# Routed experts in a fused attention, mixture-of-experts and MLP kernel: experts ranked by their rows, four of them as 128-row tiles of plain fp32 products

## The chip, the cores and the metric

One core of a Trainium2 chip runs the whole kernel. The metric is the device time of one execution in microseconds; lower is better. Engines are named as in the profile: PE (TensorE products; PEld its weight loads), DVE (VectorE), ACT (ScalarE), POOL (GpSimd), SP (SyncE, which here only issues DMAs).

## The reference

Three stages follow each other: windowed attention with sink columns (2 batches, 8 heads, 768 positions, head size 64), a top-1 mixture of 8 experts over the 1536 rows, and an MLP with a mish-like activation. The middle one is what the change touches:

```python
e_idx = np.argmax(x @ w_gate, axis=1)              # x: 1536 x 512
for e in range(8):                                 # w1: 8 x 512 x 1024, w2: 8 x 1024 x 512
    mask = e_idx == e
    h = np.maximum(x[mask] @ w1[e], 0.0)
    out[mask] = gate_w[mask, None] * eom[mask, e, None] * (h @ w2[e])
h = out @ w_in; g = h * np.tanh(softplus(h)); return g @ w_out    # d_ff 2048
```

All is fp32. With the inputs that the reference draws, the eight experts get 290, 123, 98, 163, 117, 165, 92 and 488 rows; the first 128 rows of expert 0 are computed ahead of the others, which leaves 162 of it.

## The kernel before

**Attention and routing.** `fast()` computes the attention of a pair of heads at a time; `place` scatters each row, scaled by its gate, into a DRAM `table` with an area for each expert (POOL, L337). `rank` leaves `left`, the rows of each expert that are still to be done. On DVE L845 to L891 then pick the expert with the most rows, put it last, and make the integer tables `uni` (weight offsets, table row and output position of each unit) and `lasti`. Meanwhile `pre_chunk` computes 128 rows of expert 0 by plain fp32 products (L790, L798) and splits expert 0's weights (L212 on ACT, L214 on DVE). Then all engines branch on `more`, the number of tiles beyond the planned ten (0 here).

**Experts.** `experts_and_mlp` runs ten tiles of 192 rows: units 0 to 6 have one tile, unit 7, the largest, three. A fp32 product is made of three fp32r products: weights and rows are each split into a high and a low part (ACT copies to fp32r, DVE subtracts: L1117 and L1111 for weights, `split_x` for rows). In `tile_mm` each weight block of 128x128 is used twice: its high part with 384 columns (rows' high and low, L956 and L973), its low part with 192 (L959, L975). `first(b)` makes two blocks of the hidden layer, `second(b)` adds them into `Y`; `put` copies `Y` to `yT`.

**Weights.** A unit's weights are eight pieces of 512 KB: RAW[0..3] are 128 rows of w1 (rows of 4 KB), RAW[4..7] 256 rows of w2 (rows of 2 KB). Each tile has eight `slot`s; the list `jobs` says which piece is split in which slot. `low()` subtracts the low part of the piece before, and then `fetch` loads the same piece of the next unit into the RAW buffer that is now free. SP issues DMAs strictly in the order written. The order of PE, ACT and DVE is written out by hand (`manual_schedule`).

**MLP.** For each of 48 blocks, `in_mm` does 12 products into one bank of a two-bank tile H2, `sigm` (L1254) is the first of the activation's steps on ACT, and `out_mm` (L1231) follows three blocks later. The first two blocks run inside the last tile.

Of the kernel before, what the change touches and what calls it, by code (L numbers as in the profile page):

```python
# [12 lines left out]
F32 = mybir.dt.float32  # L13
# [10 lines left out]
P = 128  # L24
# [3 lines left out]
E = 8  # L28
# [12 lines left out]
NX = 7  # L41
# [3 lines left out]
def tile_kernel(  # L45
# [103 lines left out]
    nc.gpsimd.iota(cap7, [[W, NX]], base=W, channel_multiplier=0, allow_small_or_imprecise_dtypes=True)  # L149
# [616 lines left out]
    W2S += pairs4(wp, "wc")  # L766
    psH = ctx.enter_context(tc.tile_pool(name="mpsH", bufs=1, space=PSUM))
# [9 lines left out]
    def pre_chunk():  # L777
# [29 lines left out]
        place(1, 3, NB - 3, True)  # L807
        hps.append(bank2()[:, 0])
# [23 lines left out]
    with tc.manual_schedule(engines={ET.PE, ET.Activation, ET.DVE}):  # L832
# [7 lines left out]
        extra = mid.tile([P, E], F32, name="extra")  # L840
        em = mid.tile([P, 1], F32, name="em")
        big = mid.tile([P, 1], F32, name="big")
        cd = mid.tile([P, E], F32, name="ecd")
        isem = const.tile([P, E], F32, name="isem")
        v_.tensor_reduce(big, left[:, 1:E], AX.X, ALU.max)  # L845
        v_.scalar_tensor_tensor(cd[:, 1:E], left[:, 1:E], big, id8[:, 1:E], ALU.is_ge, ALU.mult)
        v_.tensor_reduce(em, cd[:, 1:E], AX.X, ALU.max)
        v_.tensor_scalar(big, big, float(W), None, ALU.is_gt)
        v_.scalar_tensor_tensor(em, em, float(1 - E), big, ALU.add, ALU.mult)
        v_.tensor_scalar(em, em, float(E - 1), None, ALU.add)  # L850
        v_.tensor_scalar(isem, id8, em, None, ALU.is_equal)
        key = mid.tile([P, E], F32, name="key")
        v_.scalar_tensor_tensor(key, isem, float(E), id8, ALU.mult, ALU.add)
        v_.tensor_tensor(t64, key.unsqueeze(2).to_broadcast([P, E, E]), key.unsqueeze(1).to_broadcast([P, E, E]),
                         ALU.is_gt)
        v_.tensor_tensor(t64, t64, tot.unsqueeze(1).to_broadcast([P, E, E]), ALU.mult)
        v_.tensor_reduce(off, t64, AX.X, ALU.add)
        v_.tensor_tensor(st_, off, early, ALU.add)
        need = const.tile([P, E], F32, name="need")
        v_.scalar_tensor_tensor(need, isem, -float((LT_ - 1) * W), left, ALU.mult, ALU.add)  # L860
        v_.tensor_tensor(m7, need.unsqueeze(2).to_broadcast([P, E, NX]), cap7.unsqueeze(1).to_broadcast([P, E, NX]),
                         ALU.is_gt)
        v_.tensor_reduce(extra, m7, AX.X, ALU.add)
        v_.tensor_reduce(big, extra, AX.X, ALU.add)
        v_.tensor_copy(cnti, big)
        stc = const.tile([P, E], F32, name="stc")
        v_.tensor_copy(stc, st_)
        ext = const.tile([P, E], F32, name="ext")
        v_.tensor_copy(ext, extra)
        eu = mid.tile([P, E], F32, name="eu")  # L870
        v_.scalar_tensor_tensor(eu, id8, em, id8, ALU.is_ge, ALU.add)
        v_.tensor_copy(eu[:, E - 1:E], em)
        unf = mid.tile([P, E, 4], F32, name="unf")
        v_.tensor_scalar(unf[:, :, 0], eu, float(DM), None, ALU.mult)
        v_.tensor_scalar(unf[:, :, 1], eu, float(FF), None, ALU.mult)
        v_.tensor_scalar(unf[:, :, 2], eu, float(CAP), None, ALU.mult)
        v_.tensor_tensor(t64, id8.unsqueeze(1).to_broadcast([P, E, E]), eu.unsqueeze(2).to_broadcast([P, E, E]),
                         ALU.is_equal)
        v_.tensor_tensor(t64, t64, st_.unsqueeze(1).to_broadcast([P, E, E]), ALU.mult)
        v_.tensor_reduce(unf[:, :, 3], t64, AX.X, ALU.add)  # L880
        v_.tensor_copy(unf[:, 0, 3:4], st_[:, 0:1])
        v_.tensor_copy(uni, unf)
        rl = mid.tile([P, LT_], F32, name="rl")
        v_.tensor_tensor(cd, isem, left, ALU.mult)
        v_.tensor_reduce(big, cd, AX.X, ALU.add)
        v_.tensor_scalar(big, big, -float(W), 0.0, ALU.add, ALU.max)
        v_.tensor_scalar(rl, cap7[:, 0:LT_], -float(W), big, ALU.add, ALU.min)
# [11 lines left out]
    def experts_and_mlp(extra):  # L899
# [6 lines left out]
        rows = rest.enter_context(tc.tile_pool(name="rows", bufs=1))  # L906
        nrm = [rows.tile([P, 512, 2], I32, name=f"nr{c}") for c in range(2)]
        nt = [rows.tile([P, 512], F32, name=f"nt{c}") for c in range(2)]
# [10 lines left out]
        HW = W // 2  # L919
        XS = xp.tile([P, NP, 2, W], F32R, name="XS")  # L920

        def load_x(row, xr=None):
            if xr is None:
                xr = xrp.tile([HW, 2, DM], F32, name="xr")
            first["x"] = nc.sync.dma_start(out=xr, in_=table[ds(row, W), :].rearrange("(p t) f -> p t f", t=2))
            return xr

        def split_x(xr):
            pt = bank2()
            for t in range(2):  # L930
                for d in range(NP):
                    nc.tensor.transpose(pt[:, t, d * HW:(d + 1) * HW], xr[:, t, d * P:(d + 1) * P], ident[0:HW, 0:HW])  # L932
            xs_ = XS.rearrange("p d s (c t) -> p d s t c", t=2)
            pv_ = [pt[:, t, 0:NP * HW].rearrange("p (d c) -> p d c", c=HW) for t in range(2)]
# [5 lines left out]
        def put(pos):  # L940
            for c in range(2):
                t = tb.tile([P, 2, W], F32, name="t")
                nc.scalar.activation(t, Y[c][:, :, W:2 * W], AF.Copy)
                nc.vector.tensor_tensor(yT[:, 2 * c:2 * c + 2, ds(pos, W)], Y[c][:, :, 0:W], t, ALU.add)

        def tile_mm(w1s, w2s, nxt, slot):

            hT = {}

            def first(b, i):  # L950
                hp = bank2()
                for f in range(2):
                    fb = 2 * b + f
                    c = slice(fb * P, (fb + 1) * P)
                    for d in range(NP):
                        nc.tensor.matmul(hp[:, f, 0:2 * W], lhsT=w1s[d][0][:, c], rhs=XS[:, d].rearrange("p s c -> p (s c)"),  # L956
                                         start=(d == 0), stop=False, skip_group_check=True)
                    for d in range(NP):
                        nc.tensor.matmul(hp[:, f, 0:W], lhsT=w1s[d][1][:, c], rhs=XS[:, d, 0],  # L959
                                         start=False, stop=(d == NP - 1), skip_group_check=True)  # L960
                t = tb.tile([P, 2, W], F32, name="t")
                hs = hT[b] = hb.tile([P, 2, 2, W], F32R, name="hs")
                nc.scalar.activation(t, hp[:, :, W:2 * W], AF.Copy)  # L963
                nc.vector.tensor_tensor(t, hp[:, :, 0:W], t, ALU.add)  # L964
# [34 lines left out]
        xr0 = xrp.tile([HW, 2, DM], F32, name="xr")  # L999
        def extra_tiles():  # L1000
# [39 lines left out]
            pick(sj, stc)  # L1040
            v_.tensor_scalar(exf[:, :, 0], ej, float(DM), None, ALU.mult)
            v_.tensor_scalar(exf[:, :, 1], ej, float(FF), None, ALU.mult)
# [3 lines left out]
            v_.scalar_tensor_tensor(exf[:, :, 2], ej, float(CAP), rj, ALU.mult, ALU.add)  # L1046
            v_.tensor_copy(exi, exf)

            def one(j):
                at = [value(exi[0:1, j, c:c + 1], [ET.SP], c) for c in range(3)]  # L1050
                pos = value(exi[0:1, j, 3:4], [ET.DVE], 3)
                xr = load_x(at[2], xr0)
# [4 lines left out]
                split_x(xr)  # L1057
                tile_mm(W1[1], W2S, lambda: None, lambda i: None)
                put(pos)
# [13 lines left out]
        load_x(P, xr0)  # L1073
# [11 lines left out]
        split_x(xr0)  # L1085
# [7 lines left out]
        jobs = []  # L1093
        for t, (u, k_) in enumerate(TILES):
            if u < E - 1:
                jobs += ([(u, p_) for p_ in (5, 6, 7)] if u else [None] * 3) + [(u + 1, p_) for p_ in (0, 1, 2, 3, 4)]
            elif k_ == 0:
                jobs += [(u, p_) for p_ in (5, 6, 7)] + [None, ("n", NA), None, ("n", NA + 1), ("n", NA + 2)]
            elif k_ < LT_ - 1:
                jobs += [("n", NA + 3)] + [(E, p_) for p_ in range(3)] + [("n", NA + 4), (E, 3), ("n", NA + 5), None]  # L1100
# [336 lines left out]
```

## Time and profile before

| | |
|---|---|
| median of 3 runs | 656.57 us (656.41 to 656.68) |
| the profiled execution | 654.65 us, of which the span from first to last instruction is 652.9 |
| PE busy | 610.9 us, 94% of the span |
| tile 0 begins / tile 1 / tile 5 / tile 6 / tile 9 | 173.43 / 194.79 / 270.94 / 290.33 / 347.73 us |
| MLP alone on PE | from 371.74 us |
| DMA traffic | 81.05 MB |

A row of the timeline gives start, duration, engine, line, operation, output<-inputs, shapes and a count; brackets give the engine's idle time just before and what ended it. A merged row covers several instructions. PEclk is the granted TensorE clock: 1.00 is 2.4 GHz, 0.50 is 1.2 GHz.

### The profile page before, as it was taken

The numbers are of one execution on the slowest core, as the hardware profiler recorded it, in microseconds if no ns is written. First come the engines' busy times: TensorE is split into PE (matmuls) and PEld (weight loads), VectorE is DVE, ScalarE is ACT, GpSimd is POOL, SyncE is SP. The second block draws the span as 40 slices with busy tenths as digits, with TensorE's granted clock in tenths as the row PEclk, the third lists the DMA queues.
The fourth block names the chain that finished last, engine by engine and source line by source line (L and its number), as shares of the span: only waits on it lengthen the run. The fifth ranks groups of instructions, "written<-read, shape, count | busy, mean of one in ns | idle before, by whom it ended". The sixth has DMA issues, their size and how long they took to land.

```text
span 652.9 us, 9634 instructions
## 1 busy us (share of the span) xinstructions
PE 610.9 (94%) x3460; PEld 501.8 (77%) x3460; DVE 382.4 (59%) x841; ACT 410.9 (63%) x748; POOL 46.5 (7%) x73
## 2 busy tenths in 40 slices
PE   3999999889599999999999989999899999999995
PEld 2556666565499999999999867777688887888884
DVE  4466669659368788888887777677323133231312
ACT  2666666548167667666455776868767576766752
POOL 3020113304000000000000000000020000200002
PEclk9999999999699999999999989999999999999998
DMA  6789796502668777778331113221010000100001
GB/s 127 180 209 318 223 278 198 186 17 98 222 231 264 248 238 237 254 233 263 118 99 64 65 64 112 81 97 35 1 65 0 1 0 1 64 2 0 2 0 70
DMA packets 66000, 81.05 MB, mean 124 GB/s; under 512 B 42832, under 2 KB 42832, under 8 KB 65936
## 3 DMA queue, kind: packets, MB, share of 16 engines
q1 hardware_dynamic: 63872, 73.97, 37.1%
q0 software_dynamic: 1920, 6.29, 2.4%
q8 instruction: 32, 0.52, 0.3%
q14 instruction: 32, 0.26, 0.2%
q10 hardware_dynamic: 144, 0.00, 0.0%
HBM read 66.88 MB, written 13.37 MB: 123 GB/s over the span
## 4 chain that ended last, share of the span: by engine, by line
PE 65%; issue 15%; DVE 8%; ACT 6%; DMA 2%; POOL 1%; SPq 0%; POOLq 0%; DVEq 0%; ACTq 0%
PE h L1216 14%; PE acc L1231 12%; PE h L956 9%; PE Y L973 8%; PE h L959 5%; PE Y L975 4%; PE pt L305 3%; PE s L308 3%; PE avA L308 3%; DMA nr<-in_moe_w_in_dram 2%; PE pt L308 1%; DVE ms L526 1%; POOL out_dram L1245 1%; PE h L932 1%; ACT p L528 1%
## 5 line engine op out<-in xcount | busy, mean ns | idle before, releaser
L1263 DVE TENSOR_TENSOR fx<-h,fx 128x512 f32<-128x512 f32 x48 | 31.0, 687 | 140.0 <-ACT fx L1260 140.0
L973 PE MATMUL Y<-hs,wch 128*128 128x384 f32 x320 | 94.5, 361 | 0.0
L975 PE MATMUL Y<-hs,wcl 128*128 128x192 f32 x320 | 80.6, 252 | 0.0
L1254 ACT ACTIVATE fx<-h,nln 128x512 f32<-128x512 f32 x48 | 33.1, 689 | 68.5 <-PE h L1216 68.3
L528 ACT ACTIVATE p<-ms,nm 128x272 f32<-128x272 f32 (+1 forms) x96 | 47.3, 494 | 30.8 <-DVE nm L526 30.1
L975 PEld LDWEIGHTS Y<-hs,wcl 128*128 128x128 f32 x320 | 61.1, 191 | 0.1
L973 PEld LDWEIGHTS Y<-hs,wch 128*128 128x128 f32 x320 | 60.1, 188 | 0.1
L526 DVE CUSTOM_DVE_ANT_0 ms<-s,m 128x272 f32<-128x272 f32 (+1 forms) x96 | 36.3, 408 | 23.5 <-PE s L308 19.1
L963 ACT ACTIVATE t<-h 128x384 f32<-128x384 f32 x40 | 19.7, 493 | 42.2 <-PE h L959 41.1
L1216 PE MATMUL h<-yh,wah 128*128 128x512 f32 x96 | 39.0, 406 | 7.4 <-ACT fx L1254 7.4
L1245 POOL DMA_INDIRECT out_dram<-nr,idx x12 | 11.5, 961 | 475.2 <-DVE nr L1241 472.5
L956 PE MATMUL h<-XS,wbh 128*128 128x384 f32 x192 | 42.7, 344 | 0.1
L308 PE MATMUL s<-kT,qT 64*128 64x272 f32 (+1 forms) x192 | 40.0, 454 | 2.1 <-DVE nm L526 2.1
L1216 PE MATMUL h<-yh,wal 128*128 128x512 f32 x96 | 38.5, 401 | 0.0
L1231 PE MATMUL acc<-wdh,gh 128*128 128x512 f32 x96 | 38.0, 395 | 0.0
L1231 PE MATMUL acc<-wdl,gh 128*128 128x512 f32 x96 | 37.9, 394 | 0.0
L964 DVE TENSOR_TENSOR t<-h,t 128x384 f32<-128x384 f32 x40 | 22.3, 557 | 25.7 <-ACT t L963 24.8
L1111 DVE TENSOR_TENSOR wcl<-rax,wch 128x1024 fp32r<-128x1024 f32 x30 | 36.5, 1215 | 0.0
L556 ACT ACTIVATE ph<-pt 128x512 f32<-128x512 f32 (+1 forms) x48 | 24.9, 550 | 16.8 <-PE pt L305 16.8
L1267 ACT ACTIVATE gh<-fx 128x512 fp32r<-128x512 f32 x48 | 29.5, 632 | 5.7 <-DVE fx L1263 5.7
L1271 DVE TENSOR_TENSOR gl<-fx,gh 128x512 fp32r<-128x512 f32 x48 | 31.0, 689 | 2.4
L1117 ACT ACTIVATE wch<-rax 128x1024 fp32r<-128x1024 f32 x30 | 31.7, 1058 | 0.8 <-PE Y L973 0.8
(277 smaller groups left out, 1455.9 us busy)
## 6 DMA issues: line engine op xcount, KB each, us to landing
rax<-in_moe_w_dram SPq DMA_DIRECT2D x56, 512.0 KB, 4.6
nr<-in_moe_w_in_dram SPq DMA_DIRECT2D x16, 512.0 KB, 5.8
nr<-in_moe_w_out_dram SPq DMA_DIRECT2D x16, 512.0 KB, 3.5
table<-zer SPq DMA_DIRECT2D x17, 256.0 KB, 5.9
raw<-in_moe_w_dram SPq DMA_DIRECT2D x8, 512.0 KB, 5.7
xr<-table SPq DMA_DIRECT2D x10, 384.0 KB, 7.1
vr<-in_v_dram SPq DMA_DIRECT2D x16, 192.0 KB, 3.6
kr<-in_k_dram SPq DMA_DIRECT2D x14, 192.0 KB, 3.9
```

Of the source, the lines that this page charges most:

```text
L308: last_pe[0] = nc.tensor.matmul(*args, **kw)
L526: nc.vector.tensor_tensor_reduce(ms[:, 0:w], s[j][:, 0:w], m, 1.0, 3.0e38, ALU.add, ALU.min, nm[:, j, i:i + 1])
L528: nc.scalar.activation(p[:, j, i, o:o + w], ms[:, 0:w], AF.Exp, bias=nm[:, j, i:i + 1], scale=-1.0, accum_out=sm[:, j, i:i + 1])
L956: nc.tensor.matmul(hp[:, f, 0:2 * W], lhsT=w1s[d][0][:, c], rhs=XS[:, d].rearrange("p s c -> p (s c)"), start=(d == 0), stop=False, skip_g ...
L959: nc.tensor.matmul(hp[:, f, 0:W], lhsT=w1s[d][1][:, c], rhs=XS[:, d, 0], start=False, stop=(d == NP - 1), skip_group_check=True)
L973: nc.tensor.matmul(Y[c // 2][:, c % 2, 0:2 * W], lhsT=wh, rhs=hT[b][:, f].rearrange("p s c -> p (s c)"), start=(b == 0 and f == 0), stop=F ...
L975: nc.tensor.matmul(Y[c // 2][:, c % 2, 0:W], lhsT=wl, rhs=hT[b][:, f, 0], start=False, stop=(b == 3 and f == 1), skip_group_check=True)
L1111: nc.vector.tensor_tensor(lo, RAW[p_], hi.bitcast(F32), ALU.subtract)
L1117: nc.scalar.activation(wpair(*j)[0], RAW[j[1]], AF.Copy)
L1216: nc.tensor.matmul(h, lhsT=wt[:, (fb % 8) * P:(fb % 8 + 1) * P], rhs=xx[d], start=(k_ == 0), stop=(k_ == 11))
L1231: nc.tensor.matmul(accs[tb], lhsT=g_[:, tb * P:(tb + 1) * P], rhs=w_[:, c], start=(fb == 0 and k_ == 0), stop=(fb == NF - 1 and k_ == 2))
L1254: nc.scalar.activation(x_, st[n]["h"], AF.Sigmoid, bias=nln2)
```

## The change

The units are ranked on the chip by their rows (`rank_e`): unit 0 stays expert 0, then the others in ascending order; unit 7 is the largest. Units 1 to 4 (`SM`) get one tile of 128 rows each, units 0, 5 and 6 one of 192, unit 7 two of 192 and a last one of 128. Units 1 to 4 are computed by `tile_plain`: plain fp32 products straight from RAW, no splits, and each piece is fetched anew for the next unit as soon as its products are issued. For them a w1 piece is a block of 256 columns of all 512 rows, so that its DRAM runs are 1 KB. The splits of unit 5 move into tile 4. The rows of tile 0 are loaded before the branch (`load_x` in `pre_chunk`). In the MLP the odd block's `in_mm` is told not to depend on the even block's `sigm`. Output positions and ids are made in tiles 0 to 2 rather than 2 to 5. POOL makes a few more small constants at the start.

```diff
+SM = range(1, 5)
+    nrm = [rows.tile([P, 512, 2], I32, name=f"nr{c}") for c in range(2)]
+    xr0 = nrm[0].bitcast(F32).rearrange("p f w -> p (f w)")
...
         place(1, 3, NB - 3, True)
+        load_x(P, W, xr0)
...
+        v_.scalar_tensor_tensor(key, left, float(E), kb, ALU.mult, ALU.add)
+        v_.tensor_tensor(t64, rows_of(key), cols_of(key), ALU.is_gt)
+        v_.tensor_reduce(rank_e, t64, AX.X, ALU.add)
+        v_.tensor_tensor(hot_r, rows_of(id8), cols_of(rank_e), ALU.is_equal)
...
+            elif unit in SM and p < 4:
+                nc.sync.dma_start(out=RAW[p].rearrange("p (d f) -> p d f", d=NP),
+                                  in_=w1f[ds(wat[unit][0], DM), p * 256:(p + 1) * 256].rearrange("(d p) f -> p d f", p=P))
...
+        def tile_plain(u, nxt, slot):
+            def first(b, i):
+                hp = bank2()
+                w_ = RAW[b].rearrange("p (d f) -> p d f", d=NP)
+                for f in range(2):
+                    for d in range(NP):
+                        nc.tensor.matmul(hp[:, f, 0:P], lhsT=w_[:, d, f * P:(f + 1) * P], rhs=XT[:, d],
+                                         start=(d == 0), stop=(d == NP - 1), skip_group_check=True)
+                hT[b] = tb.tile([P, 2, W], F32, name="t")
+                nc.scalar.activation(hT[b][:, :, 0:P], hp[:, :, 0:P], AF.Relu)
+                slot(i)
+                fetch(u + 1, b)
+            def second(b):
+                for f in range(2):
+                    for c in range(NP):
+                        nc.tensor.matmul(Y[c // 2][:, c % 2, 0:P], lhsT=RAW[4 + b][:, f * 512 + c * P:f * 512 + (c + 1) * P],
+                                         rhs=hT[b][:, f, 0:P], start=(b == 0 and f == 0), stop=(b == 3 and f == 1),
+                                         skip_group_check=True)
+                fetch(u + 1, 4 + b)
+            slot(0)
+            first(0, 1)
+            first(1, 2)
+            second(0)
+            first(2, 3)
+            second(1)
+            first(3, 4)
+            slot(5)
+            nxt()
+            second(2)
+            slot(6)
+            second(3)
+            slot(7)
...
-        load_x(P, xr0)
+            load_x(P, W, xr0)
...
+        wide = [P if u in SM or k_ == LT_ - 1 else W for u, k_ in TILES]
+        jobs = {(4, 3 + p_): (5, p_) for p_ in range(5)}
+        for u in (5, 6, 7):
+            jobs.update({(u, i_): (u, 5 + i_) for i_ in range(3)})
+            if u < 7:
+                jobs.update({(u, 3 + p_): (u + 1, p_) for p_ in range(5)})
...
+                if n % 2:
+                    tc.declare_no_dep(mm.ins, st[n - 1]["sg"].ins, reason="the two banks of one tile")
...
+            if u in SM:
+                tile_plain(u, nxt, slot)
+            else:
+                tile_mm(wide[t], W1[u % 2], W2S, nxt, slot)
```

## Rows read from the trace of the kernel before

**Rows 1.** The page, part 1: busy time, share of the span, instructions.

```profile
PE 610.9 (94%) x3460; PEld 501.8 (77%) x3460; DVE 382.4 (59%) x841; ACT 410.9 (63%) x748; POOL 46.5 (7%) x73
```

**Rows 2.** Windows: busy us by engine, PEclk, DMA share, GB/s; tiles 1-4, MLP.

```profile
194.79:270.94 76.15, 76.15 (x547) 76.15 (x545) 64.40 (x97) 52.66 (x80) 0.00 (x0) 1.00 0.79 250
374.70:649.00 274.30, 264.03 (x1117) 209.80 (x1116) 111.29 (x181) 186.43 (x261) 11.53 (x12) 0.99 0.10 34
```

**Rows 3.** Timeline, PE: first product of tiles 0, 1, 5, 6, 9.

```profile
173.43 0.66 PE L956 MATMUL h<-XS,wah 128*128 128x384 f32 x1 [1.40 <-ACT yT L1089]
...
194.79 0.36 PE L956 MATMUL h<-XS,wbh 128*128 128x384 f32 x1
...
270.94 0.36 PE L956 MATMUL h<-XS,wbh 128*128 128x384 f32 x1
...
290.33 0.36 PE L956 MATMUL h<-XS,wah 128*128 128x384 f32 x1
...
347.73 0.41 PE L956 MATMUL h<-XS,wbh 128*128 128x384 f32 x1
```

**Rows 4.** Timeline, PE: plain fp32 products and transposes back to back.

```profile
144.81 0.73 PEld L308 LDWEIGHTS pt<-wx,xT 128*128 128x128 f32 x5
...
145.49 0.49 PEld L305 LDWEIGHTS pt<-ident,xpre 128*128 128x128 f32 x4
...
159.34 3.60 PE L798 MATMUL h<-raw,zer 128*128 128x512 f32 x8
```

**Rows 5.** The chain of work: twelve split (fp32r) products of 512 columns.

```profile
386.06 2.80 PE h L1216 x12
```

**Rows 6.** Windows as in Rows 2: loads in runs of 256 B, then of 2-4 KB.

```profile
10.00:12.00 2.00, 1.41 (x7) 1.00 (x5) 0.00 (x0) 0.49 (x1) 0.00 (x0) 1.00 1.12 249
176.00:182.00 6.00, 6.00 (x35) 6.00 (x35) 1.68 (x3) 1.85 (x4) 0.00 (x0) 0.81 1.04 404
```

**Rows 7.** Pieces of weights: ns of a split's halves; landing of a piece.

```profile
L1117 ACT ACTIVATE wbh<-rax x18: 1047/1052/1059, 183.2 to 366.2; 128x1024 fp32r<-128x1024 f32 x18
...
L1111 DVE TENSOR_TENSOR wbl<-rax,wbh x18: 1203/1219/1223, 185.2 to 377.2; 128x1024 fp32r<-128x1024 f32 x18
...
DMA to landing us min/median/max: 3.5/4.6/9.3
```

**Rows 8.** Timeline: first and last of 36 routing instructions on DVE; the branch.

```profile
150.22 0.15 DVE L845 TENSOR_REDUCE big<-left 128x1 f32<-128x7 f32 x1
...
156.75 0.17 DVE L891 CAST lasti<-lsf 128x6 int32<-128x6 f32 x1
...
161.70 4.63 DVE L214 TENSOR_TENSOR wcl<-raw,wch 128x1024 fp32r<-128x1024 f32 x4
...
166.24 0.69 DVE L1070 COPY nt<-h 128x512 f32<-128x512 f32 x1
166.47 0.35 SPq L925 DMA_DIRECT2D xr<-table  x1
169.05 2.19 SPq L193 DMA_DIRECT2D rax<-in_moe_w_dram  x4
...
169.66 1.51 PE L932 MATMUL h<-ident,xr 96*128 96x96 f32 x8 [6.72 <-DMA xr<-table]
...
172.20 1.02 DVE L938 TENSOR_TENSOR XS<-h,XS 128x384 fp32r<-128x384 f32 x2 [5.27 <-ACT XS L936]
```

**Rows 9.** Windows as in Rows 2: the two stretches at the lower clock.

```profile
168.10:178.30 10.20, 7.24 (x30) 6.90 (x31) 1.02 (x2) 1.64 (x4) 0.00 (x0) 0.50 0.84 290
379.70:383.10 3.40, 3.40 (x10) 2.62 (x9) 3.26 (x7) 0.63 (x1) 0.00 (x0) 0.50 0.39 139
```

**Rows 10.** Waits of PE's weight loads from 374 us (total, times, longest); timeline.

```profile
PEld h L1216 <- ACT fx L1254: 10.9, 9, 4.4
...
378.66 0.50 PE L1216 MATMUL h<-yh,wah 128*128 128x512 f32 x1 [3.94 <-ACT fx L1254]
```

**Rows 11.** Timeline: the first work of PE in the span.

```profile
9.25 0.87 PE L305 MATMUL pt<-ident,kr 128*128 128x128 f32 x3 [9.25 <-DMA kr<-in_k_dram]
```

More of the change, by code (lines that the diff above doesn't have):

```diff
@@ L766, in tile_kernel, with load_x @@
     W2S += pairs4(wp, "wc")
+    rows = ctx.enter_context(tc.tile_pool(name="rows", bufs=1))
+    nrm = [rows.tile([P, 512, 2], I32, name=f"nr{c}") for c in range(2)]
+    nt = [rows.tile([P, 512], F32, name=f"nt{c}") for c in range(2)]
+    xr0 = nrm[0].bitcast(F32).rearrange("p f w -> p (f w)")
+    def load_x(row, w, xr):
+        return nc.sync.dma_start(out=xr[0:w // 2].rearrange("p (t f) -> p t f", t=2),
+                                 in_=table[ds(row, w), :].rearrange("(p t) f -> p t f", t=2))
     psH = ctx.enter_context(tc.tile_pool(name="mpsH", bufs=1, space=PSUM))
@@ L856, in tile_kernel @@
[L856 removed]
+        one1 = mid.tile([P, 1], F32, name="one1")
+        key = mid.tile([P, E], F32, name="key")
+        rank_e = mid.tile([P, E], F32, name="rank_e")
+        hot_r = mid.tile([P, E, E], F32, name="hot_r")
+        over = mid.tile([P, E], F32, name="over")
+        eu, stu, lu, ext = [const.tile([P, E], F32, name=n_) for n_ in ("eu", "stu", "lu", "ext")]
+        unf = mid.tile([P, E, 4], F32, name="unf")
@@ L918, in experts_and_mlp, with halves, split_x @@
         tb = moe.enter_context(tc.tile_pool(name="tb", bufs=3))
[L919 to L929, printed above, removed]
+        XS = xp.tile([P, NP * 2 * W], F32R, name="XS")
+        XT = xp.tile([P, NP, P], F32, name="XT")
+        def halves(w):
+            return XS[:, 0:NP * 2 * w].rearrange("p (d s c) -> p d s c", d=NP, s=2)
+        def split_x(xr, w):
+            pt, hw = bank2(), w // 2
             for t in range(2):
                 for d in range(NP):
-                    nc.tensor.transpose(pt[:, t, d * HW:(d + 1) * HW], xr[:, t, d * P:(d + 1) * P], ident[0:HW, 0:HW])
-            xs_ = XS.rearrange("p d s (c t) -> p d s t c", t=2)
-            pv_ = [pt[:, t, 0:NP * HW].rearrange("p (d c) -> p d c", c=HW) for t in range(2)]
+                    nc.tensor.transpose(pt[:, t, d * hw:(d + 1) * hw], xr[0:hw, t * DM + d * P:t * DM + (d + 1) * P],
+                                        ident[0:hw, 0:hw])
+            xs_ = halves(w).rearrange("p d s (c t) -> p d s t c", t=2)
+            pv_ = [pt[:, t, 0:NP * hw].rearrange("p (d c) -> p d c", c=hw) for t in range(2)]
             for t in range(2):
@@ L938, in split_x, with turn_x, put, put_plain @@
                 nc.vector.tensor_tensor(xs_[:, :, 1, t], pv_[t], xs_[:, :, 0, t].bitcast(F32), ALU.subtract)
-        def put(pos):
+        def turn_x(xr):
+            pt = bank2()
+            for d in range(NP):
+                nc.tensor.transpose(pt[:, 0, d * P:(d + 1) * P], xr[:, d * P:(d + 1) * P], ident)
+            nc.scalar.activation(XT, pt[:, 0].rearrange("p (d c) -> p d c", c=P), AF.Copy)
+        def put(w, *to):
             for c in range(2):
                 t = tb.tile([P, 2, W], F32, name="t")
-                nc.scalar.activation(t, Y[c][:, :, W:2 * W], AF.Copy)
-                nc.vector.tensor_tensor(yT[:, 2 * c:2 * c + 2, ds(pos, W)], Y[c][:, :, 0:W], t, ALU.add)
-        def tile_mm(w1s, w2s, nxt, slot):
+                nc.scalar.activation(t[:, :, 0:w], Y[c][:, :, w:2 * w], AF.Copy)
+                for pos, a, z in to:
+                    nc.vector.tensor_tensor(yT[:, 2 * c:2 * c + 2, ds(pos, z - a)], Y[c][:, :, a:z], t[:, :, a:z], ALU.add)
+        def put_plain(pos):
+            for c in range(2):
+                nc.vector.tensor_copy(yT[:, 2 * c:2 * c + 2, ds(pos, P)], Y[c][:, :, 0:P])
+        def tile_mm(w, w1s, w2s, nxt, slot):
             hT = {}
+            xs_ = halves(w)
             def first(b, i):
@@ L1056, in one @@
                     split((W1[1] + W2S)[p_], RAW[p_], p_, nc.vector)
-                split_x(xr)
-                tile_mm(W1[1], W2S, lambda: None, lambda i: None)
-                put(pos)
+                split_x(xr0, W)
+                tile_mm(W, W1[1], W2S, lambda: None, lambda i: None)
+                put(W, (pos, 0, W))
                 if j + 1 < NX:
@@ L1295, in start, with stow @@
                 late[-1][0]()
-        ASIDE = {(2, 7): places, (3, 7): split_places, (4, 1): lambda: hot_of_places(0),
-                 (4, 5): lambda: hot_of_places(1), (5, 1): blocks_of_places}
+        ASIDE = {(0, 2): second_place, (0, 4): places, (1, 1): split_places, (1, 2): lambda: hot_of_places(0),
+                 (1, 4): lambda: hot_of_places(1), (2, 1): blocks_of_places}
         was = [None]
+        def stow(t):
+            at_ = [value(x_, [ET.DVE], 3) for x_ in was[0]]
+            if t == 0:
+                put(W, (at_[0], 0, P), (at_[1], P, W))
+            elif TILES[t][0] in SM:
+                put_plain(at_[0])
+            else:
+                put(wide[t], (at_[0], 0, wide[t]))
         for t, (u, k_) in enumerate(TILES):
@@ L1336, in nxt @@
             def nxt():
-                if not last:
-                    split_x(xr1)
+                if not last and u1 in SM:
+                    turn_x(xr1)
+                elif not last:
+                    split_x(xr1, wide[t + 1])
                 elif not extra:
@@ L1352, in experts_and_mlp @@
                 x_[1]()
-        put(value(was[0], [ET.DVE], 3))
+        stow(NTL - 1)
         if extra:
```

186 lines of the change are left out of this document (90 added, 96 removed).

## Prediction

> **What bounds the kernel now.** First I read the page's busy times: PE is busy for 94% of the span [rows 1], so time can only go where PE's work shrinks, where its clock rises, or where one of its few waits goes. Then the windows by stage: in tiles 1 to 4 PE never rests, at the full clock, while the DMAs move 250 GB/s [rows 2]. The first products of the tiles give the price of a tile [rows 3]: tiles 1 to 4 take 270.94 - 194.79 = 76.15 us, 19.04 each; tile 5 takes 19.39 (the ids' products are in it); tile 0 takes 21.36. Tile 0 is longer because its first part runs at 1.2 GHz: PE had rested before it, and PEclk is 0.50 from 168.1 to 178.3 [rows 9]. The two rests are visible: before tile 0 PE waits 6.72 us for the tile's rows, which SP asks for only at 166.47 [rows 8]; in the MLP, PE waits for the sigmoid nine times, 10.9 us in all, the longest 3.94 on PE itself, and that one again costs a stretch at half clock [rows 9, 10].
>
> **The change, part by part.** The sum is made against the profiled execution, 654.65 us (span 652.9 and 1.75 around it); the median of the runs shown is 656.57, so 1.92 goes on top of the result.
>
> **Products of a 128-row tile.** None of the before kernel's lines is a plain product of 128x128 by 128, so its price is bounded by neighbours: transposes of that shape follow each other after (0.49 - 0.14)/3 = 0.12 us, 160-column products after (0.73 - 0.19)/4 = 0.135, 512-column ones after (3.60 - 0.59)/7 = 0.43 [rows 4]; 0.43 is 0.84 ns a column, which for 128 gives 0.107. I take 0.111 (between). A tile has 32 products in `first` and 32 in `second`, plus 4 transposes: 68 x 0.111 = 7.5 us of PE instead of 19.04. The Trainium skill (FP8 and Floating Point Precision, TensorE Precision Notes) says that true fp32 takes four passes through the array. Rows speak for two: the same 512 columns cost 0.43 us plain [rows 4] and 2.80/12 = 0.233 us as fp32r [rows 5]; four passes would make the tile about 14 us (rival 3).
>
> **What is late next: the weights.** A plain tile eats its 4.19 MB with no split between, so in the steady state a tile lasts as long as its loads. A RAW buffer is asked for again right after its eight products (0.9 us), in the order in which it will be needed, so I count the DMA queue as never empty from tile 1 on. The rate with full queues is 404 GB/s in runs of 2 to 4 KB, and 249 in runs of 256 B [rows 6]. w2 (2.10 MB, 2 KB runs): 5.2 us. w1 in 1 KB runs is in no row: 5.2 us at 404, 8.4 at 249; 1 KB is one doubling from 2 KB and two from 256 B, so I take 350 GB/s, 6.0 us. The tile's rows (0.26 MB) 0.7 to 1.3, taken 1.1. Sum D = 12.3 us a tile (11.1 to 14.9).
>
> **From tile 1 to tile 5.** Let T1 be the start of tile 1, with all of unit 1 loaded. The first fetch leaves at T1 + 1.2; the shortest landing is 3.5 us for a piece whose transfer is 1.3 [rows 6, 7], so 2.2 is latency. Units 2, 3 and 4 are in at T1 + 1.2 + 2.2 + 3 x 12.3 = T1 + 40.3; tile 4 ends about 1 us later. Unit 5 is again a split tile and needs all four w1 pieces split before its first block is whole. Its rows (0.39 MB) take 1.3, its pieces 1.3 each, in the order 0, 1, 4, 2, 5, (6,0), 3: SP's list has `fetch(6, 0)`, which waits for the low half of (5, 0), ahead of `fetch(5, 3)`, because `slot(4)` stands before it in `first(3)`. So piece 3 is seventh: 40.3 + 1.3 + 9.1 = 50.7; its halves take 1.05 on ACT and 1.22 on DVE [rows 7]: 53.0; the products ahead of the one that needs it are worth 1.1. Tile 5 begins, in effect, at T1 + 51.9 instead of T1 + 76.15: gain 24.2 (16.5 to 27.8 for D from 14.9 to 11.1). PE rests for some 10 us before tile 5, longer than both rests before, so tile 5 starts at half clock; the two earlier stretches held 3.4 us and about 5 us of gapless products [rows 3, 9], that is 1.7 to 2.5 us lost, taken 2.5. The ids' 0.34 us (19.39 - 19.05) leave tile 5 for tile 2, where PE waits for DMAs anyway. Tile 5: loss 2.2.
>
> **Before tile 0.** The rows' load now waits on SP only for the last scatter; behind it on SP stand the branch's register reads and unit 1's loads, which before could not leave until DVE had let go of the old weights either (169.05, after the 166.33 end of the last low half [rows 8]). DVE's routing list shrinks from 36 to 26 instructions at (156.92 - 150.22)/36 = 0.19, 1.9 us, of which I keep 1.1, since the low halves also wait for ACT. So the low halves end at about 165.2. From the first transpose to the first product it took 173.43 - 169.66 = 3.77 [rows 3, 8]; if the chain starts only at 165.2, tile 0 begins at 169.1; if only DVE's copy and subtraction (0.69 and 1.02 [rows 8]) are left, at 167.2. I take 168.5, gain 4.9 (3.2 to 6.2). PE's rest shrinks from 7 us to about 3, and whether the clock still falls is open: tile 0 takes 19.05 to 21.36, taken 20.2. Tile 1 thus begins at 188.7, 6.1 earlier (3.2 to 8.5). Unit 1's loads, 12.5 us from about 167, are in by 182.
>
> **The last tile** is 128 wide: a pair of products costs (19.04 - 0.6)/64 = 0.288 now; with 256 and 128 columns hardly under twice 0.111, taken 0.236 (half of 0.233 and a little, and 0.111). 64 x 0.052 = 3.3 (0 to 4.5): its ACT and DVE work shrinks with it, except that of the weights.
>
> **The MLP.** Without the dependence, an odd block's 12 products can follow at once. The 10.9 us of waits go, and the 3.4 us at half clock become 1.7 [rows 9, 10]. What is late next is the second half of the activation, needed by `out_mm` three blocks on; ACT is busy 186 of 274 us and DVE 111 [rows 2], so I give back 1.3. Gain 11.3 (6 to 12.6).
>
> **At nothing.** POOL's some 15 new constants (0.1 to 0.2 us each) hide behind the first DMA, PE starting only at 9.25 [rows 11]; without cover 2 us. Positions and ids on DVE move to tiles that have lost their splits. `xr0` shares a buffer that is next loaded in tile 6.
>
> Sum: 6.1 + 24.2 - 2.2 + 3.3 + 11.3 = 42.7; 654.65 - 42.7 = 611.95 for the profiled execution, 613.9 for the median, said as 614.
>
> **Rivals.** (1) *As above*, 614, with own range 608 to 620: chance 0.50. (2) *The 1 KB runs are slow.* At the rate of the 256 B runs D is 14.9, tile 5 at T1 + 59.7: 622 (618 to 628). For it: the runs are the only new kind of load; against: 2 KB runs reach the full rate. 0.20. (3) *PE bounds the plain tiles*, because products cost double, either since the clock falls between the bursts or since the plain product is dearer than its neighbours. Products at 0.22 make a tile 14.6 us; the last of four ends at about T1 + 55 (the first at full clock), unit 5's pieces come with tile 4's pace and land by then, and tile 5 starts at T1 + 56 without a rest: 614 + 4.1 - 2.5 = 616, or 618 with some rest. For it: PE fell to half clock after both rests [rows 9]; against: the rests within a plain tile are under 1 us each. The Trainium skill (TensorE: Matmul & The Clock Gate, HAM oscillation) describes just this: short bursts with DMA waits between them run cold each time. Its example has waits of 3 to 5 us; the trace agrees in so far as both falls stand at rests of 4 us and more. 0.12. (4) *The MLP's wait moves rather than goes*: `out_mm` waits for the activation instead, gain 4: 621. 0.07. (5) *Better*: D = 11.1 and no clock loss: 606. 0.06. (6) *Slower than before.* If one of the four smallest counts exceeded 128, an extra tile would run ahead: 13.4 us for its eight pieces, 10 for their splits, 19 of products, 10 to bring expert 0's back, and the MLP's first blocks no longer inside the last tile, 6: 614 + 58 = 672. It decides from the 129th row on; the counts are 92, 98, 117 and 123, the middle ones 163 and 165 (limit 192), so this needs other inputs. 0.03, which also stands for a stall in the loads that I don't see. That the ranked order does nothing at all (same counts in another order) is no case of its own: the tiles' width is fixed in the program. 0.02 is left for no change.
>
> **Numbers.** The likeliest case gives 614. From 604 to 630 the range takes in (1) to (5) and the bounds of D, of the start and of the MLP. About 0.2% is what a measurement of this kernel can tell from no change; faster by more 0.95, within it 0.02, slower 0.03.
>
> **What would show it.** Plain products follow at about 0.11 us; tiles 2 to 4 are about 12.3 us apart with PE waiting for DMA in each; the DMAs run near 360 GB/s there; PE rests about 10 us before tile 5, released by the split of piece (5, 3), and PEclk is 0.50 after it; tile 0 begins at 168 to 169; no MLP product waits for a sigmoid. I am wrong if tile 4 ends late because of PE rather than DMA, if the rest before tile 5 is short, or if `out_mm` waits.

## The result, and the profile of the changed kernel

The changed kernel takes 625.75 us, median of four runs (624.41 to 627.0), against 656.58 before: a ratio of 0.953 (0.951 to 0.955). The forecast was 614 with 604 to 630: right in sign and inside the range, but 12 us too low, and outside the 608 to 620 that the likeliest case had for itself. The profiled execution of the changed kernel takes 625.45 us, of which 623.6 is the span.

Part 1 of the page shows what [rows 1] showed: PE is still busy for 94% of a span that is 29 us shorter, while DVE and ACT lost 57 and 44 us of work.

```profile
PE 588.7 (94%) x3444; PEld 482.0 (77%) x3444; DVE 325.4 (52%) x766; ACT 366.5 (59%) x688; POOL 48.3 (8%) x88
```

The windows (columns as in Rows 2) are of tiles 1 to 4, tile 5, the MLP, and the half-clock stretch around tile 0:

```profile
193.85:254.35 60.50, 59.90 (x546) 59.57 (x545) 10.67 (x28) 12.32 (x26) 0.00 (x0) 1.00 0.87 286
254.35:275.69 21.34, 19.59 (x136) 19.11 (x137) 17.34 (x25) 14.68 (x21) 0.00 (x0) 1.00 0.94 302
355.90:620.00 264.10, 260.39 (x1118) 209.10 (x1116) 111.19 (x181) 187.16 (x262) 11.54 (x12) 1.00 0.10 36
167.05:177.30 10.25, 6.59 (x28) 6.25 (x29) 1.79 (x4) 1.40 (x3) 0.00 (x0) 0.50 0.85 279
```

The first row speaks against my main step at once: in tiles 1 to 4 PE is busy for 59.90 of 60.50 us at the full clock. DVE and ACT have fallen to a fifth of [rows 2], and it brought PE no wait for DMA, because PE itself has nearly as much to do as the tile lasts. Why is seen in the timeline of PE (columns as in Rows 3): the transposes of tile 0's rows and its first product, two stretches of plain products in tile 3, the start of tile 5 with its waits, then tile 6, four rows of the last tile and the first product of the MLP alone. The first row's wait is put down to SP's L1527, the call that the whole kernel is in; the rows' load, issued at 165.44, had landed after 3.4 us, at about 168.8.

```profile
169.32 1.52 PE L942 MATMUL h<-ident,nr 96*128 96x96 f32 x8 [4.39 <-SPq L1527]
...
173.08 1.62 PE L980 MATMUL h<-XS,wah 128*128 128x384 f32 x4 [1.39 <-ACT yT L1154]
...
223.97 3.74 PE L1036 MATMUL h<-XT,rax 128*128 128x128 f32 x32
227.55 1.95 PE L1046 MATMUL Y<-t,rax 128*128 128x128 f32 x16
...
254.35 0.76 PE L980 MATMUL h<-XS,wbh 128*128 128x384 f32 x3 [0.50 <-DVE XS L949]
256.35 0.44 PE L980 MATMUL h<-XS,wbh 128*128 128x384 f32 x1 [1.24 <-ACT wbh L1181]
...
257.61 0.36 PE L983 MATMUL h<-XS,wbl 128*128 128x192 f32 x1 [0.51 <-DVE wbl L1175]
...
275.69 0.88 PE L980 MATMUL h<-XS,wah 128*128 128x384 f32 x4
...
332.95 0.66 PE L980 MATMUL h<-XS,wbh 128*128 128x256 f32 x4
...
338.45 0.33 PE L998 MATMUL Y<-hs,wch 128*128 128x256 f32 x1
338.62 0.22 PE L1000 MATMUL Y<-hs,wcl 128*128 128x128 f32 x1
338.68 0.33 PE L998 MATMUL Y<-hs,wch 128*128 128x256 f32 x1
...
353.20 0.44 PE L1290 MATMUL h<-yh,wah 128*128 128x512 f32 x1
```

`first(0)` and `first(1)` hold 16 products in the code, and the row shows 32 instructions in 227.55 - 223.97 = 3.58 us. The groups of tiles 1 to 4 by shape (operation, tiles, shapes, count | busy us, mean ns | idle before) say the same for all of them:

```profile
L1046 PE MATMUL Y<-t,rax 128*128 128x128 f32 x256 | 30.7, 275 | 0.0
L1036 PE MATMUL h<-XT,rax 128*128 128x128 f32 x256 | 30.6, 275 | 0.0
```

Four tiles with 32 products of each kind make 128, and 256 instructions are there: **a plain fp32 product is two instructions of 3.58/32 = 0.112 us**, 0.22 us in all. 64 of them and the transposes make the 14.7 to 15.6 us that a plain tile takes.

Where the 29.3 us of span went, by the first products of the stages:

| stage | before | after | gained | forecast |
|---|---|---|---|---|
| up to tile 1 | 194.79 | 193.85 | 0.9 | 6.1 |
| tiles 1 to 4 | 76.15 | 60.50 | 15.7 | 24.2 |
| tile 5 | 19.39 | 21.34 | -2.0 | -2.2 |
| tiles 6 to 8 | 57.40 | 57.26 | 0.1 | 0 |
| last tile, with two MLP blocks | 24.01 | 20.25 | 3.8 | 3.3 |
| MLP alone on PE | 281.2 | 270.4 | 10.8 | 11.3 |

### The profile page after: what moved, and what is told of

It is laid out like the page before. It is cut to its first block, busy times and chain, and to the rows that moved or that the text cites. A ratio compares the mean times of both kernels' runs of the same rounds, so it can differ in the third digit from the quotient of the medians.

```text
span 623.6 us, 9496 instructions
## 1 busy us (share of the span) xinstructions
PE 588.7 (94%) x3444; PEld 482.0 (77%) x3444; DVE 325.4 (52%) x766; ACT 366.5 (59%) x688; POOL 48.3 (8%) x88
## 4 chain that ended last, share of the span: by engine, by line
PE 44%; issue 13%; DVE 7%; ACT 6%; DMA 1%; POOL 1%; POOLq 0%; ACTq 0%
PE h L1290 10%; PE acc L1307 8%; PE Y L998 6%; PE h L980 5%; PE h L1036 5%; PE Y L1046 4%; PE h L983 3%; PE Y L1000 2%; DVE nt L245 1%; DVE nt L246 1%; ACT L1336 1%; ACT gh L1343 1%; ACT fx L1333 1%; DVE gl L1347 1%; DVE nt L244 1%
## 5 line engine op out<-in xcount | busy, mean ns | idle before, releaser
L998 PE MATMUL Y<-hs,wch 128*128 128x384 f32 (+1 forms) x192 | 54.9, 357 | 0.0
L1000 PE MATMUL Y<-hs,wcl 128*128 128x192 f32 (+1 forms) x192 | 47.1, 246 | 0.0
L1000 PEld LDWEIGHTS Y<-hs,wcl 128*128 128x128 f32 x192 | 36.7, 191 | 0.1
L998 PEld LDWEIGHTS Y<-hs,wch 128*128 128x128 f32 x192 | 36.1, 188 | 0.2
L1039 ACT ACTIVATE t<-h 128x256 f32<-128x256 f32 x16 | 6.2, 385 | 46.4 <-PE h L1036 46.4
L1046 PE MATMUL Y<-t,rax 128*128 128x128 f32 x256 | 30.7, 275 | 0.0
L1036 PE MATMUL h<-XT,rax 128*128 128x128 f32 x256 | 30.6, 275 | 0.0
```

What stands on the lines that cost most here:

```text
L998: nc.tensor.matmul(Y[c // 2][:, c % 2, 0:2 * w], lhsT=wh, rhs=hT[b][:, f].rearrange("p s c -> p (s c)"), start=(b == 0 and f == 0), stop=F ...
L1000: nc.tensor.matmul(Y[c // 2][:, c % 2, 0:w], lhsT=wl, rhs=hT[b][:, f, 0], start=False, stop=(b == 3 and f == 1), skip_group_check=True)
L1036: nc.tensor.matmul(hp[:, f, 0:P], lhsT=w_[:, d, f * P:(f + 1) * P], rhs=XT[:, d], start=(d == 0), stop=(d == NP - 1), skip_group_check=True)
L1046: nc.tensor.matmul(Y[c // 2][:, c % 2, 0:P], lhsT=RAW[4 + b][:, f * 512 + c * P:f * 512 + (c + 1) * P], rhs=hT[b][:, f, 0:P], start=(b == ...
```

## Experiments

The metric of one kernel moves by up to 5 us between executions, and the stretch ahead of the routing alone makes some 3 us of that: POOL's first scatter begins at 150.0 and 150.6 us in the two profiles with the old code there and at 150.2 to 153.2 in the eight with the new one. So small effects are read from that first scatter on, or from the starts of the tiles, in the profiles; totals are given beside the kernel before on the same chip.

### Half of the plain products

```diff
-                    for d in range(NP):
+                    for d in range(NP // 2):
...
             def second(b):
-                for f in range(2):
+                for f in range(1):
```

> The changed kernel, with half of the products of the four plain tiles left out (two of the four d in `first`, one of the two f in `second`), all loads as they are; so the outputs of experts in those tiles are not the reference's. Theory A: a plain fp32 product of 128 columns is two PE instructions of 0.111 us, 0.222 in all, so PE (64 x 0.222 + 0.45 = 14.7 us) and not the loads bounds tiles 1 to 4. Then with half the products PE needs 7.6 us a tile, the loads become the bound that my prediction had taken, D = 12.3 (11.1 to 14.9): tile 5 begins 51 to 54 us after tile 1 instead of 60.5, PE waits for DMAs in every plain tile and rests before tile 5; total 616 to 620 instead of 625.5. Rival B: the loads or the buffers' turn-around set the 14.85 us a tile already: tile 5 still begins 59 to 61 us after tile 1, total 624 to 627.

Measured: 617.07 us (615.44 to 618.92), ratio 0.941 (0.936 to 0.945). Tile 5 begins 243.42 - 191.21 = 52.2 us after tile 1. Waits for DMA stand in the plain tiles now (first two rows), and before tile 5 PE rests in two pieces:

```profile
208.72 1.09 PE L954 MATMUL h<-ident,xr 128*128 128x128 f32 x4 [2.93 <-DMA xr<-table]
...
228.00 1.13 PE L1046 MATMUL Y<-t,rax 128*128 128x128 f32 x8 [0.27 <-DMA rax<-in_moe_w_dram]
...
235.49 1.51 PE L942 MATMUL h<-ident,xr 96*128 96x96 f32 x8 [4.93 <-DMA xr<-table]
...
243.42 1.30 PE L980 MATMUL h<-XS,wbh 128*128 128x384 f32 x3 [3.65 <-DVE XS L949]
```

The windows (columns as in Rows 2) of 20 us in the middle of the loads, of the stretch right behind them where unit 5's loads begin, and of tile 5:

```profile
208.00:228.00 20.00, 17.52 (x132) 16.81 (x133) 2.13 (x8) 3.76 (x10) 0.00 (x0) 0.83 1.07 366
230.00:234.00 4.00, 0.55 (x5) 0.36 (x4) 0.00 (x0) 0.00 (x0) 0.00 (x0) 0.76 1.05 229
243.40:265.80 22.40, 21.80 (x136) 21.09 (x137) 17.53 (x25) 14.59 (x21) 0.00 (x0) 0.87 0.92 293
```

Theory A holds. With PE's work halved, the kernel does what I had forecast for the change itself: full queues move 366 GB/s in runs of 1 and 2 KB, which makes (4.19 + 0.26)/0.366 = 12.2 us a tile (my D was 12.3); PE rests before tile 5; and the clock falls there (PEclk 0.87 over tile 5, which lasts 22.4). The slow 1 KB runs of rival 2 are ruled out too.

### 128-row tiles of split products

```diff
+PLAIN = ()
...
-            elif TILES[t][0] in SM:
+            elif TILES[t][0] in PLAIN:
...
-        jobs = {(4, 3 + p_): (5, p_) for p_ in range(5)}
-        for u in (5, 6, 7):
+        jobs = {(0, 3 + p_): (1, p_) for p_ in range(5)}
+        for u in range(1, 8):
...
-            if u in SM:
+            if u in PLAIN:
                 tile_plain(u, nxt, slot)
```

> The changed kernel with units 1 to 4 still as 128-row tiles, but of split products (three fp32r products in two instructions, as in the other tiles), w1 pieces in 4 KB runs again, and the splits back in their slots. Theory A: what shortened the tiles is the width 128 in place of 192, not the missing splits: in the last tile of the changed kernel the two instructions of a weight block take 0.229 us at this width, a plain product 0.222. Then 64 x 0.229 + 0.5 = 15.2 us a tile, tile 5 begins 60 to 63 us after tile 1 (60.5 in the changed kernel), and tile 5 keeps its 19.4 us since its splits are done ahead (21.3 in the changed kernel): total 623 to 627, the same as the changed kernel's. Rival B: the plain products are what brought the gain, and the splits on ACT and DVE (13 and 16 us a tile at 192 columns) bound the tile again: tiles 1 to 4 take 17 to 19 us each, tile 5 begins 68 to 76 us after tile 1, total 633 to 640.

Measured: 623.43 us (622.16 to 625.19), ratio 0.950 (0.946 to 0.955). The window of tiles 1 to 4 (192.18 to 254.24):

```profile
192.18:254.24 62.06, 62.06 (x558) 61.64 (x557) 57.63 (x97) 47.51 (x81) 0.00 (x0) 1.00 0.91 292
```

Tiles 1 to 4 take 62.1 us instead of 60.5, all of it PE at the full clock, and tile 5 takes 19.06 instead of 21.34, since its splits are done ahead: together 81.1 against 81.8. Theory A holds: **the narrower tile is what gained, and the plain products gained nothing**. The work on DVE (57.63 of 62.06 us) is back and costs nothing, since PE ends last.

### The count for the branch made later

```diff
-        v_.tensor_copy(cnti, one1)
...
         parts(1, 2)
+        nc.vector.tensor_copy(cnti, one1)
         first(1, 2, 4)
```

> The changed kernel, with one cast on DVE moved: `cnti`, which every engine reads for the branch, is made after the second split of `pre_chunk` instead of within the routing. POOL then issues all six scatters ahead of its read of `cnti`; before, that read stood between the third and the fourth. Theory A: the rows of tile 0 come late because POOL waited there for DVE's `cnti`, which stands later in the new routing list (4.3 us after the list's start instead of 3.4): the last three scatters follow at once, the rows' load leaves 2 to 3 us earlier after the routing's start, tile 0 and all after it begin 2 to 3 us earlier, total 622.5 to 624. Rival B: the scatters are slow by themselves (1.8 and 2.0 us instead of 1.0, while DVE does wide subtractions), or the chain of the low halves ends last anyway: tile 0 less than 0.7 us earlier, total 625 to 626.

Measured: 621.91 us (620.64 to 624.04), ratio 0.948 (0.944 to 0.953). The timeline of POOL (columns as in Rows 3), first of the changed kernel, then of this one, the third to the sixth scatter:

```profile
155.16 0.96 POOL L351 DMA_INDIRECT table<-xs,rowi  x1 [0.30 <-issue]
158.06 1.78 POOL L351 DMA_INDIRECT table<-xs,rowi  x1 [1.95 <-DVE lasti L907]
160.15 1.97 POOL L351 DMA_INDIRECT table<-xs,rowi  x1 [0.30 <-issue]
162.42 1.09 POOL L351 DMA_INDIRECT table<-xs,rowi  x1 [0.30 <-ACT wch L226]
```

```profile
153.18 0.96 POOL L351 DMA_INDIRECT table<-xs,rowi  x1 [0.30 <-issue]
154.44 0.96 POOL L351 DMA_INDIRECT table<-xs,rowi  x1 [0.30 <-issue]
155.71 0.96 POOL L351 DMA_INDIRECT table<-xs,rowi  x1 [0.30 <-issue]
156.98 0.96 POOL L351 DMA_INDIRECT table<-xs,rowi  x1 [0.30 <-ACT zer L817]
```

From the first scatter to the last it is 6.4 us instead of 9.9, from the first scatter to the rows' load 9.3 instead of 12.9, and to tile 0 16.4 instead of 20.5: the start gains 4.2 us, more than expected. Theory A holds, but what B said of slow scatters has a share: of the 3.6 us by which the load leaves earlier, 1.65 are the wait ahead of the fourth scatter and the rest is that the last three take 0.96 us each instead of 1.78, 1.97 and 1.09.

Of the 4.2 us, tiles 4 and 5 give 2.6 back (16.86 and 22.71 instead of 15.64 and 21.34), for two reasons. In the timeline of PE, the start of tile 5, and in the windows (columns as in Rows 2) of the whole tile 5 and of two microseconds in it:

```profile
248.89 0.76 PE L980 MATMUL h<-XS,wbh 128*128 128x384 f32 x3 [1.72 <-DVE XS L949]
250.76 0.45 PE L980 MATMUL h<-XS,wbh 128*128 128x384 f32 x1 [1.11 <-ACT wbh L1181]
...
252.02 0.53 PE L983 MATMUL h<-XS,wbl 128*128 128x192 f32 x1 [0.50 <-DVE wbl L1175]
```

```profile
248.89:271.60 22.71, 21.10 (x136) 20.61 (x137) 17.52 (x25) 14.59 (x21) 0.00 (x0) 0.92 0.92 291
253.00:255.00 2.00, 2.00 (x9) 2.00 (x9) 0.76 (x1) 0.22 (x1) 0.00 (x0) 0.50 1.06 325
```

At the end of tile 4 PE waits 1.72 us for the split rows instead of 0.50, because unit 5's w1 pieces, which ACT splits ahead of the rows, come later (ACT waits 2.13 and 1.51 us for them, in the changed kernel at most 0.27): from 234 to 238 us the DMAs are busy for 92% and move 259 GB/s, at the same place of tile 4 in the changed kernel 283. In tile 5 itself the waits are no longer than there (1.11 and 0.50 us against 1.24 and 0.51); its 1.4 us more are the clock, which falls to 0.50 behind these short rests. From the first scatter to the end of the span 2.8 us are won.

### The next unit's fetch ahead of the slot

```diff
-                slot(i)
                 fetch(u + 1, b)
+                slot(i)
```

> The changed kernel with the two lines at the end of `first` in a plain tile exchanged: the fetch for the next unit stands ahead of `slot`, so that SP issues piece 3 of unit 5 ahead of piece 0 of unit 6. Theory A: tile 5 is 1.95 us longer than before the change because PE waits 2.9 us for the split of piece 3, which was the seventh load instead of the sixth; one piece earlier is 1.3 us: tile 5 takes 19.7 to 20.3 us instead of 21.3, total 1 to 1.5 us less. Rival B: the piece comes late for another reason (PE's products with the old contents of its buffer end late, so the load cannot leave earlier): tile 5 still takes 21.0 to 21.5.

Measured: 623.71 us (622.82 to 623.95), ratio 0.950 (0.945 to 0.954). Tile 5 lasts 20.65 us instead of 21.34. The order of SP's list does cost something, but half of what theory A said: a piece earlier is 0.7 us here, and PE still waits for the split of piece 3, only less (0.55 instead of 1.24 us; with the old order and whole products it is 1.11 us with the count late and 1.06 with the rows behind the branch). Neither theory had the size.

### The MLP's edit alone, in the kernel before

```diff
+                if n % 2:
+                    tc.declare_no_dep(mm.ins, st[n - 1]["sg"].ins, reason="the two banks of one tile")
```

> The kernel before with one edit of the change alone: the odd block's products in the MLP are told not to depend on the even block's sigmoid. Theory A: the waits for the sigmoid (10.9 us) and the half-clock stretch behind the longest of them go, and PE finds its next work at once: the MLP alone on PE takes 270.4 us as in the changed kernel instead of 281.2, total 10.3 to 11.3 us under the kernel before, a ratio of 0.983. Rival B: the wait moves to `out_mm`, or part of the gain in the changed kernel comes from its narrower last tile (ACT reaches the MLP earlier): gain 4 to 9 us.

Measured: 646.2 us (643.56 to 648.84) against 657.14, ratio 0.985 (0.982 to 0.988). From the last product of the tiles to the end of the span it is 270.8 us; before it was 281.3 and in the changed kernel 270.5. What stands in place of [rows 10] in the waits of PE from 374 us (total, times, longest), and the window of the MLP as in [rows 2]:

```profile
PEld h L1216 <- ACT yh L1189: 1.4, 4, 0.7
PEld h L1216 <- DVE yl L1190: 0.3, 1, 0.3
PE h L1216 <- ACT yh L1189: 0.3, 1, 0.3
PEld acc L1233 <- DVE gl L1273: 0.3, 1, 0.3
```

```profile
374.00:640.00 266.00, 261.12 (x1117) 208.69 (x1115) 111.32 (x181) 186.45 (x261) 11.54 (x12) 1.00 0.11 37
```

No wait for the sigmoid is left, `out_mm` (L1233) waits once for 0.3 us, and the clock is 1.00 throughout. Theory A holds: the edit gives 10.5 us by itself and owes nothing to the last tile.

### The rows loaded behind the branch again

```diff
-        load_x(P, W, xr0)
         hps.append(bank2()[:, 0])
...
+        load_x(P, W, xr0)
         wat = {
```

> The changed kernel with one step undone: tile 0's rows are loaded behind the branch again, into the same buffer as in the changed kernel. Theory A: the earlier load is what brought tile 0 forward; undone, the load leaves SP some 15.9 us after POOL's first scatter as in the kernel before (12.9 in the changed kernel), tile 0 begins 22 to 23 us after that scatter instead of 20.5, total 627 to 628. Rival B: the branch itself costs SP nothing by then (SP has long taken it), the load is held by the last scatter's landing alone, and what held it in the kernel before was its buffer: load and tile 0 within 0.5 us of the changed kernel's, total 625 to 626.

Measured: 627.21 us (624.95 to 629.35) against 657.14, ratio 0.955 (0.951 to 0.959). The first scatter and the rows' load, in the timelines of POOL and SP:

```profile
153.21 1.04 POOL L351 DMA_INDIRECT table<-xs,rowi  x1 [15.00 <-DVE key L881]
...
166.08 0.35 SPq L788 DMA_DIRECT2D nr<-table  x1
```

The load leaves 12.87 us after the first scatter, as in the changed kernel (165.44 - 152.56 = 12.88), and tile 0 begins 20.3 us after it (20.5). Rival B holds: the place of the load gains nothing, since it waits for the last scatter either way. In the kernel before it left 15.9 us after the first scatter, 0.1 us after the last low half [rows 8]. What SP's queue waited for there (total, times, longest), first in the kernel before, then in the changed one, says why:

```profile
SPq L925 <- DMA table<-xs,rowi: 6.6, 1, 6.6
SPq L925 <- DVE wcl L214: 5.1, 1, 5.1
```

```profile
SPq L788 <- DMA table<-xs,rowi: 7.8, 1, 7.8
```

Before, the load waited for the last scatter and then 5.1 us more for DVE's subtraction of the old weights; in the new buffer that second wait is gone, with the load on either side of the branch. No run put the old buffer back alone.

Tile 5 takes 22.19 us here, 0.85 more than in the changed kernel, though it runs the same code: PEclk is 0.92 over the tile, behind waits of 0.70 and 1.06 us.

### Two combinations

The late count with split tiles, and the late count with the fetch ahead of the slot.

> The count made late (as in the run where POOL issues all six scatters at once) together with the 128-row tiles made of split products. Theory A: both hold by themselves, since the split tiles have their pieces loaded a tile ahead: tile 0 begins 16.4 us after the first scatter, tile 5 begins 61.5 to 62.5 us after tile 1 and lasts 19.1; total 618.5 to 620.5. Rival B: the earlier start is given back to the loads of unit 1 or 2, which leave SP no earlier: tiles 1 and 2 wait for splits, total 621 to 623.5.

> The count made late together with the exchanged lines (fetch ahead of slot) in the plain tiles. Theory A: tile 0 begins 16.4 us after the first scatter, tile 5 lasts 20.5 instead of 21.3: total 620 to 622. Rival B: the plain tiles' loads are so near to their limit that the earlier start is mostly waited for at tile 5, as in the run with the count late alone (tile 4 and tile 5 together 2.6 us longer): total 622 to 624.

Measured against the same 657.14: 619.68 us (619.1 to 620.64), ratio 0.944 (0.941 to 0.946), and 618.23 us (617.61 to 622.59), ratio 0.943 (0.939 to 0.947). In both, tile 0 begins 16.4 us after the first scatter. With split tiles, tiles 1 to 4 take 62.1 and tile 5 takes 19.07, as theory A had it. With plain tiles they take 61.2 and 20.30: less is given back than with the late count alone (PEclk stays at 1.00 in tile 5), and the total lies below what either theory gave. From the first scatter to the end of the span the two take 465.7 and 465.5 us, the changed kernel 471.0: both beat it, by 5.3 and 5.5 us, and between them nothing can be told apart.

## Why the prediction was right, and where it was 12 us off

The number is right by the width of the range more than by the mechanism. The likeliest case (chance 0.50) had the loads bound tiles 1 to 4 and PE rest for 10 us before tile 5; neither happened. The range went up to 630 because it took in the rivals, and one of them, with 0.12, is what came.

**The plain product: the step that failed.** I divided the 0.43 us between the starts of two instructions of [rows 4] by one product. But that row says x8 where the code has four products (`second(1, 0, 4)`): 0.43 is half a product, and a product of 512 columns cost 0.86 us, nearly four times the 0.233 of an fp32r product. The transposes that I took for neighbours misled in the same way: four in the code are x4 in the row, so a transpose is one instruction and a plain product two. The count of the row against the loop in the code would have shown it. So the Trainium skill (FP8 and Floating Point Precision, TensorE Precision Notes) was right with its four passes, and I read the rows wrongly when I set them against it. A tile is 14.7 to 15.6 us of PE, not 7.5, and the gain of tiles 1 to 4 is 15.7 us, not 24.2: 8.6 of the 13.4 us by which the sum of 42.7 missed the 29.3.

**The loads: right, but not the bound.** D = 12.3 us came out as 12.2 where PE was halved. As PE needs more, the loads end nothing in tiles 1 to 4. They do so in tile 5, where piece (5, 3) is late as worked out.

**Tile 5: right in size, wrong in cause.** The loss is 2.0 us (2.2 forecast), but not from the clock, which stays at 1.00 in this profile. PE waits 1.24 and 0.51 us for the splits, which is all of its idle time in the tile (21.34 - 19.59); the other 0.5 us over a full tile's 19.05 lie in products that count as busy. The forecast's mechanism, a lower clock at the start of tile 5, appears with half the products (22.4 us), and also with whole ones, behind rests far shorter than the 10 us forecast: PEclk is 0.92 over tile 5 with the count late (22.71 us) and with the rows behind the branch (22.19 us).

**The start.** 0.9 us instead of 6.1. Counted from the first scatter, tile 0 is 2.3 us earlier, not 4.9. The routing list shrank by 1.35 us (I had counted 1.9 and kept 1.1), but one of its results, `cnti`, now stands 4.3 us behind the list's first instruction instead of 3.4, and POOL reads it between the third and fourth scatter. I had looked at what moved on SP and not at whom the new order on DVE lets wait: the late count shows it to be worth 4.2 us at tile 0. The early load itself was worth nothing. The other 2.0 us are a later first scatter (152.56 instead of 150.59), inside the spread of the eight profiles with that code; whether the new constants on POOL have a part in it, no run tells. PE's clock fell again, as I had left open, and tile 0 takes 20.8 (20.2 forecast).

**The last tile and the MLP: right.** A pair of products costs 338.68 - 338.45 = 0.23 us (0.236 taken), gain 3.8 instead of 3.3; the MLP gives 10.8 instead of 11.3, 10.5 of it shown by that edit alone.

**The rivals.** Rival 3 (PE bounds the plain tiles) is what happened, with the dearer product and not with a falling clock: PEclk is 1.00 over tiles 1 to 4, where PE hardly rests (59.90 of 60.50 us busy). With half the products the waits reach 2.9 us, not under 1 as I had put them, and with them comes a lower clock: PEclk is 0.83 from 208 to 228 us, all of it behind the wait of 2.93 us (0.50 from 210 to 214), while behind the wait of 1.10 us it is 1.00. The oscillation in the Trainium skill (TensorE: Matmul & The Clock Gate, HAM oscillation) has the clock fall at each wait, in an example with waits of 3 to 5 us; here it fell at one of the two. Rival 3 had 14.6 us a tile, but its sum was wrong: four such tiles and the ids end at T1 + 59, not 55, and the waits at tile 5 come on top. With both mended it would have said 621. Rival 5's 606 is 2 us off its own terms (3 x 1.2 us of D and 2.5 us of clock under 614 make 608). Rivals 2, 4 and 5 fell; the inputs keep rival 6 away.

The other 1.6 us between forecast and result go the other way: I had added 1.92 for the distance of the profiled execution to the median, and here it is 0.3.

## What to carry to other kernels

Before a row's time is divided by its count, hold the count against the loop in the code: an operation may be several instructions. When a change does two things at once (here narrower tiles and plain products), price each with the other left as it was; at 128 columns the two instructions of a split block take 0.23 us and those of a plain product 0.22, so all of the gain lay in the width, and the missing splits only freed engines that did not end last. When a list of small instructions is rewritten, look for the engine that reads a result from the middle of it, and for what stands in its queue behind that read.

## What the runs showed of the hardware

- A plain fp32 product of 128x128 by 128 is two PE instructions, each with a weight load of its own, 0.112 us apiece at the full clock: 0.87 ns a column in each.
- A scatter that begins while DVE does a wide subtraction (128x1024, 1.22 us) lasts until after that subtraction. The subtractions on DVE, in the changed kernel and with the count late:

```profile
157.78 1.23 DVE L228 TENSOR_TENSOR wal<-raw,wah 128x1024 fp32r<-128x1024 f32 x1 [0.23 <-issue]
...
160.06 1.22 DVE L228 TENSOR_TENSOR wal<-raw,wah 128x1024 fp32r<-128x1024 f32 x1
```

```profile
155.81 1.22 DVE L228 TENSOR_TENSOR wal<-raw,wah 128x1024 fp32r<-128x1024 f32 x1 [0.23 <-issue]
156.96 1.28 DVE L228 TENSOR_TENSOR wal<-raw,wah 128x1024 fp32r<-128x1024 f32 x1
```

  In the changed kernel the scatters of 158.06 and 160.15 us begin 0.28 and 0.09 us into such a subtraction and end at 159.84 and 162.12, 0.83 and 0.84 us after its end. All 17 scatters of the ten profiles that begin 0.09 us or more inside one end 0.82 to 0.84 us after it, whether they take 1.07 or 1.97 us. With the count late, the scatters of 155.71 and 156.98 us begin 0.10 us ahead of a subtraction and 0.02 us from the start of one, overlap them, and take 0.96. No run was made to test this by itself.
- Full queues do not always move 366 to 404 GB/s: with half the products, the 4 us from 230 on moved 229 GB/s at a DMA share of 1.05, and the 4 us from 198 on in the kernel before 248 at 0.99. What makes such a stretch, and what it costs PE, was not tried. The window of the kernel before (columns as in Rows 2):

```profile
198.00:202.00 4.00, 4.00 (x31) 4.00 (x30) 3.79 (x6) 3.03 (x6) 0.00 (x0) 1.00 0.99 248
```

- The granted clock can fall without a long rest: with the count late PE rested 1.72, 1.11 and 0.50 us within 5 us, and the clock went from 1.00 to 0.50; in the changed kernel, at the same place, rests of 0.50, 1.24 and 0.51 us left it at 1.00.
